# Retention attention with a mixture of experts: turned rows sent two chunks at a time, last outputs evicted by ScalarE alone, leftover rows turned in TensorE's waits, both quarters of w1 fetched ahead of x

## The chip, the cores and the metric

The kernel runs on one core of one Trainium2 chip. The metric is the device time of an execution in microseconds (us), the median of several runs. Before the change it is 405.49 us, median of 3 runs (405.27 to 405.95).

## What is computed

The reference is a chunk of recurrent attention with a decay for each head, and behind it a layer of eight experts that each take exactly 384 of the 3072 tokens.

```python
# B, H, S, D = 4, 8, 768, 64
for t in range(S):
    state = gamma[None, :, None, None] * state + einsum('bhd,bhe->bhde', k[:, :, t], v[:, :, t])
    y[:, :, t] = scale * einsum('bhd,bhde->bhe', q[:, :, t], state)
x = y.transpose(0, 2, 1, 3).reshape(3072, 512)
...
# N, D, E, F = 3072, 512, 8, 1024; cap = 384
logits = x @ w_gate
order = argsort(-logits.flatten())     # greedy: best (token, expert) pair first
for idx in order:                      # a token goes to an expert that has room
    ...
for e in range(E):
    mask = assigned == e
    out[mask] = relu(x[mask] @ w1[e]) @ w2[e]
```

## The kernel before, in words

**Stage 1, attention (0 to about 86 us).** The sequence is cut into 6 chunks of 128 tokens; a unit is one batch entry and one chunk, unit i = b + 4c, 24 in all. Groups of units (four single ones, then pairs, numbered g = 0 to 13) go through `scores`, `outputs`, `mix` and `states`. `mix` ends with the unit's output in PSUM, `yp`, channels on partitions and tokens along the free axis, and evicts it into `ys`: ScalarE (ACT) alone for chunks 0 to 4 (L419), ScalarE for one half and VectorE (DVE) for the other in the last chunk (L416, L417). Two things use `ys`. `gate(c)` multiplies the four units of a chunk with the gate's weights (L496, 32 matmuls) and ScalarE copies the logits to `gs` (L498). And the rows of x have to stand in DRAM, in `xs`, token by token, from where the experts gather them.

**Turned rows.** Units 0 to 16 (TURNED = 17) are turned by VectorE in blocks of 32 x 32 (`block_rows`, L466), so many behind each group as the table BLOCKS says, and sent by SyncE (SP): `send` (L473) issues four transfers, one for each 32 partitions. Chunks 0 to 2 of a batch entry lie in one buffer `x4` and go together (`send_long`, 16 transfers of 192 KB behind group 10), units 12 to 16 one by one (`send_one`, 20 transfers of 64 KB). Units 17 to 23 are turned by TensorE (`row_part`, L441, four 128 x 128 transposes into PSUM), evicted by ScalarE into one of four buffers `xr` (`row_out`, L449 and L451), and sent by SP as one transfer of 256 KB (L453): three of them by `early_rows`, around the last gate, and four by `rows_out`, behind the first step of the search.

**Stage 2, the choice of expert 0 (about 86 to 100 us).** For the last chunk the gate's logits are turned back (L630), VectorE takes each token's best expert (`m`, `oh`), compares with a grid of 64 thresholds (`cmp`), TensorE counts tokens over each threshold (pairs of columns, `by_two`), and VectorE narrows the grid twice, then finds the threshold (`code`, `Wq`) and the list of the expert's tokens (`idx`). `fill` issues matmuls on constants (L706) in TensorE's waits, FILL = (4, 7) of them in two places.

**Stage 3, the experts (from about 100 us).** GpSimd (POOL) issues indirect transfers in program order on one queue: the first quarter of expert 0's w1 half 0 (`fetch_first(0)`, L981, 0.5 MB) as soon as the expert is known, the three gathers of x (`fetch_x`, L989, 128 rows each) when `idx` is known and all rows are in DRAM, the second quarter (`fetch_first(1)`, L981), w1's half 1 (`fetch_w`, L950, 1 MB), then w2's halves (L950). TensorE turns the gathered rows (`turn_x`, L1002, tiles `pt` and `py`); ScalarE and VectorE split each operand into a high part (`xh` L1007, `w1h` L968) and a rest (`xlo`, `w1l`; every VectorE operation of a helper has line L152). `mm1` makes eight blocks f of the hidden layer (L1052, the first two of expert 0 in thirds by `by_thirds`, L1031; blocks f0 to f3 need w1's half 0, f4 to f7 half 1), `hh` and `hl` are their split results (ACT L1057, DVE), and `mm2` makes the output (L1074).

The search for the next expert goes on beside the matmuls. The order of each engine's instructions in this stage is set when the program is built by a planner: `Beside` and `Feed` keep estimated clocks for PE, DVE and POOL (`clk`), and after each group of matmuls decide which step of the search, which split of a weight and which transfer comes next. Engines then run strictly in that order.

## Time and profile before

| what | value |
|---|---|
| median of 3 runs | 405.49 us (405.27 to 405.95) |
| the profiled execution's own time | 405.79 us |
| its span, first to last instruction | 404.1 us |
| PE busy | 387.8 us, 96% of the span |
| DVE, ACT, POOL busy | 274.8, 156.6, 146.8 us |
| mean granted TensorE clock | 0.997 of full speed |

The profile is of one execution. It lies 0.30 us over the median, and 1.7 us of its time lie outside the span. PE is TensorE's matmuls, PEld its loads of weights, DVE VectorE, ACT ScalarE, POOL GpSimd, SP SyncE. The timeline's rows give start, length, engine, line, operation, tiles, and in brackets how long the engine had been idle and what ended that. A busy PE is not a PE at work on something needed: the constant matmuls of `fill` count as well.

### The profile page before, as it was taken

How to read it: one execution, taken by the hardware profiler on the slowest of the kernel's cores; microseconds unless marked ns; L12 is line 12 of the kernel's file. 1: busy time of each engine (PE TensorE's matmuls, PEld its weight loads, DVE VectorE, ACT ScalarE, POOL GpSimd, SP SyncE). 2: the span in 40 equal slices, each digit the busy share in tenths (PEclk: the TensorE clock that was granted, in tenths of full speed). 3: DMA queues.
4: the chain of work that ended last, by engine and by line, in shares of the span. 5: the costliest groups of instructions: out<-in, count | busy, mean ns of one | idle time of the engine just before them, and what ended most of it. 6: DMA issues, size and time to landing. Idle time of an engine off the chain costs nothing.

```text
span 404.1 us, 8464 instructions
## 1 busy us (share of the span) xinstructions
PE 387.8 (96%) x3452; PEld 338.4 (84%) x3453; DVE 274.8 (68%) x643; ACT 156.6 (39%) x287; POOL 146.8 (36%) x164
## 2 busy tenths in 40 slices
PE   8999999987989999999999999999999999999994
PEld 6989989964778889889988997898799889889982
DVE  5459767978979579867968895896688157156300
ACT  1422424233463265137315533353454265156210
POOL 5488783201600730161161451352256128021011
PEclk9999999999999999999999999999999999999998
DMA  7999988957753570375357373177146405710001
GB/s 282 423 415 423 401 290 263 243 128 252 219 225 104 171 298 1 116 246 213 104 148 295 131 255 161 55 222 271 53 156 226 165 33 180 334 54 26 2 26 60
DMA packets 22968, 77.50 MB, mean 192 GB/s; under 512 B 2693, under 2 KB 11655, under 8 KB 16393
## 3 DMA queue, kind: packets, MB, share of 16 engines
q0 software_dynamic: 8592, 46.14, 32.5%
q1 hardware_dynamic: 14330, 30.74, 21.3%
q8 instruction: 29, 0.48, 0.5%
q14 instruction: 17, 0.14, 0.1%
HBM read 64.29 MB, written 12.58 MB: 190 GB/s over the span
## 4 chain that ended last, share of the span: by engine, by line
PE 59%; issue 14%; DVE 12%; DMA 7%; POOL 4%; ACT 2%; POOLq 0%; SPq 0%; ACTq 0%; DVEq 0%
PE py L1074 24%; PE ph L1052 19%; DMA ld<-qkv 5%; PE yp L411 4%; PE sc L366 4%; DMA wraw<-w,wix 2%; PE pt L1002 2%; PE yp L396 2%; PE psm L152 2%; PE TP L430 1%; DVE w1l L152 1%; DVE w2l L152 1%; DVE cmp L152 1%; POOL out L1086 1%; DVE hl L152 1%
## 5 line engine op out<-in xcount | busy, mean ns | idle before, releaser
L1052 PE MATMUL ph<-xlo,w1h 128*128 128x384 f32 x256 | 81.8, 336 | 0.2 <-DVE xlo L152 0.2
L1052 PE MATMUL ph<-xh,w1h 128*128 128x384 f32 x248 | 81.8, 343 | 0.1
L1052 PE MATMUL ph<-xh,w1l 128*128 128x384 f32 x256 | 81.5, 335 | 0.0
L1074 PE MATMUL py<-w2h,hh 128*128 128x512 f32 x192 | 78.4, 408 | 0.0
L1074 PE MATMUL py<-w2l,hh 128*128 128x512 f32 x192 | 75.2, 392 | 0.4 <-DVE w2l L152 0.4
L1074 PE MATMUL py<-w2h,hl 128*128 128x512 f32 x192 | 75.1, 391 | 0.0
L1086 POOL DMA_INDIRECT out<-yo,oix x24 | 27.9, 1164 | 111.0 <-ACT yo L1084 99.7
L1057 ACT ACTIVATE hh<-ph 128x384 fp32r<-128x384 f32 x64 | 31.4, 490 | 62.0 <-PE ph L1052 61.3
L950 POOL DMA_INDIRECT wraw<-w,wix x31 | 36.4, 1175 | 43.6 <-DVE un L152 30.0
L1052 PEld LDWEIGHTS ph<-xh,w1h 128*128 128x128 f32 x248 | 46.3, 188 | 4.3 <-issue 2.7
L152 DVE TENSOR_TENSOR w1l<-wraw,w1h 128x1024 fp32r<-128x1024 f32 (+1 forms) x36 | 39.3, 1102 | 14.1 <-ACT w1h L968 14.0
L152 DVE SCALAR_TENSOR_TENSOR hl<-ph,hh 128x384 fp32r<-128x384 f32 x64 | 34.9, 553 | 19.7 <-ACT hh L1057 19.1
L1052 PEld LDWEIGHTS ph<-xlo,w1h 128*128 128x128 f32 x256 | 47.7, 188 | 0.5 <-DVE xlo L152 0.5
L1052 PEld LDWEIGHTS ph<-xh,w1l 128*128 128x128 f32 x256 | 47.6, 188 | 0.0
L989 POOL DMA_INDIRECT xg<-xs,idx x24 | 29.1, 1212 | 43.0 <-issue 32.6
L369 DVE TENSOR_TENSOR am<-sc,dm 128x512 f32<-128x512 f32 x48 | 30.0, 682 | 20.4 <-PE sc L366 20.4
L1074 PEld LDWEIGHTS py<-w2h,hl 128*128 128x128 f32 x192 | 36.1, 188 | 7.7
L1074 PEld LDWEIGHTS py<-w2l,hh 128*128 128x128 f32 x192 | 36.2, 188 | 7.1 <-DVE w2l L152 1.3
L1074 PEld LDWEIGHTS py<-w2h,hh 128*128 128x128 f32 x192 | 36.2, 188 | 5.8
L152 DVE TENSOR_TENSOR w2l<-wraw,w2h 128x1024 fp32r<-128x1024 f32 x32 | 38.6, 1218 | 1.6 <-ACT w2h L968 1.6
L1084 ACT ACTIVATE yo<-py 128x512 f32<-128x512 f32 x23 | 13.8, 600 | 60.5 <-PE py L1074 45.3
L968 ACT ACTIVATE w1h<-wraw 128x1024 fp32r<-128x1024 f32 (+1 forms) x36 | 33.5, 955 | 8.2 <-DMA wraw<-w,wix 8.2
(181 smaller groups left out, 546.7 us busy)
## 6 DMA issues: line engine op xcount, KB each, us to landing
ld<-qkv SPq DMA_DIRECT2D x20, 1024.0 KB, 12.0
ld<-qkv SPq DMA_DIRECT2D x4, 768.0 KB, 5.6
xs<-x SPq DMA_DIRECT2D x16, 192.0 KB, 4.6
xs<-xr SPq DMA_DIRECT2D x7, 256.0 KB, 2.6
xs<-x SPq DMA_DIRECT2D x20, 64.0 KB, 1.8
wraw<-w,wix POOLq DMA_INDIRECT x33, 7.7
xg<-xs,idx POOLq DMA_INDIRECT x24, 3.6
out<-yo,oix POOLq DMA_INDIRECT x24, 3.1
```

Of the source, the lines that this page charges most:

```text
L152: return f(o, *a, **k)
L366: nc.tensor.matmul(sc[s][:, pr, :], k_[r, w], q_[r, w], start=True, stop=True)
L369: masked.append(nc.vector.tensor_tensor(am[:, s], sc[s], dm[:, s], op=OP.mult))
L411: nc.tensor.matmul(yp[o:o + 64, pr, :], values(u)[:, 2 * pr + s, :], st[u][0][:, s, pr, :], start=(not c and pr == 0), stop=(pr == HP - 1) ...
L950: nc.gpsimd.indirect_dma_start(out=t, out_offset=None, in_=w1v if nm == "w1" else w2v, in_offset=bass.IndirectOffsetOnAxis(ap=wix[:, hf:hf ...
L968: nc.scalar.activation(p[0], p[2], AF.Copy)
L989: nc.gpsimd.indirect_dma_start(out=t, out_offset=None, in_=xs, in_offset=bass.IndirectOffsetOnAxis(ap=found[n][0][:, j:j + 1], axis=0))
L1052: nc.tensor.matmul(ph, a[:, o:o + 128], x_[:, d], start=(k == 0 and not begun), stop=(k == len(prods) - 1), skip_group_check=begun)
L1057: nc.scalar.activation(hh[:, f], ph, AF.Relu)
L1074: nc.tensor.matmul(py, h_[:, f, t], a[:, o:o + DM], start=(k == 0), stop=(k == 23))
L1084: nc.scalar.activation(yo, py, AF.Copy)
L1086: sct = nc.gpsimd.indirect_dma_start(out=out, out_offset=bass.IndirectOffsetOnAxis(ap=oix[:, j:j + 1], axis=0), in_=yo, in_offset=None, bo ...
```

## The change

It does these things:

1. The last chunk's outputs are evicted by ScalarE alone, one instruction of 128 x 512 for each unit, in place of a half by ScalarE and a half by VectorE.
2. Four chunks of a batch entry (units 0 to 15) go in buffers of two chunks: `send_two` issues 32 transfers of 128 KB, all behind group 10; unit 16 goes alone, in four of 64 KB. SP's sends stay 36 in number, with the same bytes. BLOCKS moves VectorE's turning forward: four units behind group 10, one behind group 12.
3. The rows of units 17 to 23 come from one generator, `rows_left`, in steps of two transposes; the first two units use PSUM tiles `yp`, the others `ph` and `py`. Steps are placed around the last gate and, by STEPS = (7, 1, 2), behind three steps of the first search. FILL falls from (4, 7) to (2, 7).
4. Both quarters of w1's half 0 are fetched by POOL as soon as the expert is known, ahead of the gathers of x; the first has a buffer of its own, `raw0`.
5. The four matmuls of block f0 on the first 128 rows move ahead of the second `turn_x`, and for the search of expert 1 VectorE, not ScalarE, negates the counts (`ng`).
6. The planner, with other clocks at its start, puts some later splits, transposes and transfers at other places.

```diff
--- before.py
+++ after.py
@@ -39,7 +39,7 @@
 WARM = (12, 0, 6)
 KNOWN = 3
 ROWBUFS = 4
-LONG = 3
+LONG = 4
 TURNED = 17
 GUESS = 4
 WINDOW = 6
@@ -48,12 +48,12 @@
 DEEP = 8
 LATER = (3, 4, 5)
 EVEN = 6
-BLOCKS = {g: 2 for g in (4, 5, 6, 7, 8, 9, 10, 12)}
-SEND = 10, 12
-COLD = 0
+BLOCKS = {4: 2, 5: 2, 6: 2, 7: 2, 8: 2, 9: 2, 10: 4, 12: 1}
+SEND = 10
+STEPS = 7, 1, 2
 HOT = 18
 THIRDS = 2
-FILL = (4, 7)
+FILL = (2, 7)
 READY0 = 0
 BITS = (6, 6, 5, 5, 5, 5)
 SHIFT = tuple(32 - sum(BITS[:i + 1]) for i in range(len(BITS)))
@@ -282,6 +282,7 @@
                   start=start, stop=stop)
+    raw0 = ctx.enter_context(tc.tile_pool(name="w0", bufs=1)).tile([128, 1024], F32, name="wraw0")
     yctx = ExitStack()
     yk = yctx.enter_context(tc.tile_pool(name="yk", bufs=1, side="right"))
     xo = yctx.enter_context(tc.tile_pool(name="xo", bufs=ROWBUFS, side="right"))
@@ -412,11 +413,7 @@
                                      start=(not c and pr == 0), stop=(pr == HP - 1), skip_group_check=True)
             YS[b, c] = (yk.tile([128, HP, C], F32, name=f"ys{b}_{c}") if b + B * c >= TURNED else
                         yk.tile([128, HP, C], F32, name="ys", bufs=9))
-            if c == NC - 1:
-                nc.scalar.activation(YS[b, c][:, 0:2], yp[:, 0:2], AF.Copy)
-                nc.vector.tensor_copy(YS[b, c][:, 2:4], yp[:, 2:4])
-            else:
-                nc.scalar.activation(YS[b, c], yp, AF.Copy)
+            nc.scalar.activation(YS[b, c], yp, AF.Copy)
     def states(us):
@@ -452,15 +449,15 @@
         t0 = (b * NC + c) * 128
         nc.sync.dma_start(xs[t0:t0 + 128, :], xr)
-    x4, x1 = {}, {}
+    x2, x1 = {}, {}
     def block_rows(i):
         b, c = units[i]
-        if not c:
-            x4[b] = rc.tile([128, LONG, 4, HP, 32], F32, name=f"x4{b}")
         if c < LONG:
-            x = x4[b][:, c]
+            if not c % 2:
+                x2[b, c // 2] = rc.tile([128, 2, 4, HP, 32], F32, name=f"x{b}_{c}")
+            x = x2[b, c // 2][:, c % 2]
         else:
             x = x1[i] = rw.tile([128, 4, HP, 32], F32, name="x1", bufs=TURNED - B * LONG)
         nc.vector.transpose(x.rearrange("p t d r -> p d t r"), YS[b, c].rearrange("p d (t r) -> p d t r", t=4))
@@ -472,21 +469,27 @@
         for g in range(4):
             nc.sync.dma_start(xv[b, g ^ 2 * (b % 2), :, 4 * c0:4 * c0 + x.shape[1]], x[32 * g:32 * g + 32])
-    def send_long():
-        for b in range(B):
-            send(b, 0, x4[b].rearrange("p c t d r -> p (c t) (d r)"))
+    def send_two():
+        for c in range(0, LONG, 2):
+            for b in range(B):
+                send(b, c, x2[b, c // 2].rearrange("p c t d r -> p (c t) (d r)"))
     def send_one(i):
         send(*units[i], x1[i].rearrange("p t d r -> p t (d r)"))
     written = []
-    def early_rows(k):
-        for i in range(len(written), len(written) + k):
-            pr_ = rp.tile([128, DM], F32, name="sc", bufs=4)
-            row_part(pr_, i, 0, HP)
+    def rows_left(tile_of):
+
+        while len(written) < len(units):
+            i = len(written)
+            pr_ = tile_of[0](i)
+            row_part(pr_, i, 0, 2)
+            yield
+            row_part(pr_, i, 2, HP)
+            written.append(i)
             row_out(pr_, i)
-            written.append(i)
+            yield
     def gate(c):
@@ -609,30 +612,30 @@
                 block_rows(len(written))
             if g > B:
                 next(chosen, None)
-            if g == SEND[0]:
-                send_long()
-            if g == SEND[1]:
-                for i in range(B * LONG, len(written)):
-                    send_one(i)
+            if g == SEND:
+                send_two()
         pc = rp.tile([128, 2 * E], F32, name="sc", bufs=4)
         early = [b * NC + c for c in (0, 2) for b in range(B)]
         for k, c in enumerate(early):
             by_two(pc, cmp0, oh0, c, k == 0, False)
         while len(written) < TURNED:
             block_rows(len(written))
-        for i in range(B * LONG + B, TURNED):
+        for i in range(B * LONG, TURNED):
             send_one(i)
-        early_rows(1)
+        left_over = [lambda i: rp.tile([128, DM], F32, name="yp", bufs=2)]
+        rows = rows_left(left_over)
+        next(rows)
         c = NC - 1
         gate(c)
-        early_rows(1)
+        next(rows)
         lt = rp.tile([128, 512], F32, name="sc", bufs=4)
         nc.tensor.transpose(lt[:, 0:128], gs[c % 2], ident)
         cols, Lc = slice(c, COLS, NC), lt[:, 0:128].rearrange("p (b x) -> p b x", b=B)[:, :, 0:E]
         f = best(Lc, cols, m0, oh0)
         reach(cols, B, m0, cmp0, th0)
         f()
-        early_rows(1)
+        next(rows)
+        next(rows)
         for b in range(B):
             by_two(pc, cmp0, oh0, b * NC + NC - 2, False, b == B - 1)
         n0 = other_half(pc, nc.vector)
@@ -762,7 +765,7 @@
                 sg = sgs[i]
                 if n or i:
                     yield
-                    pc, ng = count_pairs(cmp, oh, None if n else ve)
+                    pc, ng = count_pairs(cmp, oh, None if n > 1 else ve)
                     if n:
                         yield clk.pe + hear() + COPIED
                     full(pc, ng, sg)
@@ -792,7 +795,7 @@
             sel = sw.tile([128, COLS], BF, name="sel")
             ve.tensor_scalar(sel, a, code, None, op0=OP.is_equal)
             ve.scalar_tensor_tensor(Wq[:, 0:COLS], m, tv, sel, op0=OP.is_ge, op1=OP.mult)
-        if n == 0 and sent:
+        if n == 0:
             fill(FILL[0])
         ve.tensor_tensor_scan(Sc[:, 1:COLS + 1], Wq[:, 0:COLS], zer[:, 0:COLS], 0.0, op0=OP.add, op1=OP.add)
         wix = weight_rows(code, n)
@@ -800,9 +803,8 @@
         if n == 0:
             wix4 = mp.tile([128, 2], I32, name="wix4")
             ve.scalar_tensor_tensor(wix4, code.to_broadcast([128, 2]), -512.0, c_("wrow4"), op0=OP.mult, op1=OP.add)
-            raw["w1", 0, 0] = mp.tile([128, 2048], F32, name="wraw", bufs=5)
-            firsts["w1"] = wix4
             fetch_first(0, wix4)
+            fetch_first(1, wix4)
         if not last:
             both = sw.tile([128, 1], F32, name="both")
             ve.tensor_reduce(both, eh, axis=AX.X, op=OP.add)
@@ -817,7 +819,7 @@
         ve.scalar_tensor_tensor(s0, rk[:, 0:COLS], 32.0, Wq[:, 0:COLS], op0=OP.add, op1=OP.mult)
         if not last:
             ve.scalar_tensor_tensor(bad, rk[:, COLS:], float(CAP), bad, op0=OP.not_equal, op1=OP.max)
-        if n == 0 and sent:
+        if n == 0:
             fill(FILL[1])
         V, low = high_slots(s0, 1, n, None if n else nc.scalar)
         ob = low_slots(low)
@@ -962,7 +964,10 @@
             held.discard((nm, hf, e))
         s = slice(c0, c0 + w)
         hi, lo = wt[nm, hf]
-        return hi[:, s], lo[:, s], raw[nm, hf, e][:, s]
+        src = raw[nm, hf, e]
+        if isinstance(src, tuple):
+            src = src[c0 // 1024]
+        return hi[:, s], lo[:, s], src[:, s]
     def high_w(p):
         nc.scalar.activation(p[0], p[2], AF.Copy)
@@ -979,7 +984,7 @@
     def fetch_first(k, wix4):
         booked(("w1", 0, 0), 1456)
         nc.gpsimd.indirect_dma_start(
-            out=raw["w1", 0, 0][:, 1024 * k:1024 * k + 1024], out_offset=None,
+            out=raw["w1", 0, 0][k][:, 1024 * k:1024 * k + 1024], out_offset=None,
             in_=w1.rearrange("r (h x) -> (r h) x", h=4),
             in_offset=bass.IndirectOffsetOnAxis(ap=wix4.bitcast(U32)[:, k:k + 1], axis=0))
@@ -1091,19 +1096,6 @@
             scat.append(sct)
             yield 690
-    sent = []
-
-    def rows_out():
-        for i in range(len(written), len(units)):
-            pr_ = pp.tile([128, DM], F32, name="py" if i % 2 else "ph", bufs=2 if i % 2 else 3)
-            ns = 430 if i < len(written) + COLD else 220
-            row_part(pr_, i, 0, 2)
-            yield ns
-            row_part(pr_, i, 2, HP)
-            row_out(pr_, i)
-            yield ns
-        sent.append(True)
-
     class Beside:
@@ -1132,18 +1124,20 @@
             while n not in found:
                 self.step()
+    raw["w1", 0, 0] = raw0, mp.tile([128, 2048], F32, name="wraw", bufs=5)
     clk.dve = clk.pe = clk.pool = clk.dma = 0
     clk.busy.clear()
     side = Beside()
-    side.step()
-    for ns in rows_out():
-        side.tick(ns, -2)
+    left_over[0] = lambda i: pp.tile([128, DM], F32, name="py" if i % 2 else "ph", bufs=2 if i % 2 else 3)
+    for k in STEPS:
+        side.step()
+        for _ in range(k):
+            next(rows, None)
     side.finish(0)
     yctx.close()
     mq = ctx.enter_context(tc.tile_pool(name="mq", bufs=1, side="right", reuse_waits="tile"))
     for j in range(KT):
         fetch_x(0, j)
-    fetch_first(1, firsts.pop("w1"))
     fetch_w("w1", 1, 0, found[0][1])
     for _ in range(4):
         side.step()
@@ -1153,12 +1147,12 @@
         high_w(p)
     lows = []
     for j in range(KT):
+        if j == 1:
+            by_thirds(0, range(1))
         turn_x(0, j, lows)
-        if not j:
-            pass
-        else:
+        if j:
             side.step()
-            by_thirds(j - 1, range(THIRDS))
+            by_thirds(j - 1, range(1 if j == 1 else 0, THIRDS))
         if j < KT - 1:
             low_w(quarters[j])
         lows.pop(0)[1]()
```

On POOL, from expert 0's first weight transfer to expert 1's first (`wraw` is a weight's buffer, `xg` gathered rows, `out` the scatter of results). Before:

```order
L981 DMA wraw<-w,wix_1673 128x1024
L989 DMA xg<-xs,idx 128x512 x3
L981 DMA wraw<-w,wix_1673 128x1024
L950 DMA wraw<-w,wix 128x2048
L1170 COPY spacer<-xh 1x1
L950 DMA wraw<-w,wix 128x2048 x3
L989 DMA xg<-xs,idx 128x512 x2
L1085 MEMSET spacer 1x1
L1086 DMA out<-yo,oix 3072x512
L989 DMA xg<-xs,idx 128x512
L950 DMA wraw<-w,wix 128x2048 x2
```

After the change:

```order
L986 DMA wraw_95<-w,wix_1663 128x1024
L986 DMA wraw<-w,wix_1663 128x1024
L994 DMA xg<-xs,idx 128x512 x3
L952 DMA wraw<-w,wix 128x2048
L1164 COPY spacer<-xh 1x1
L952 DMA wraw<-w,wix 128x2048 x3
L994 DMA xg<-xs,idx 128x512
L1090 MEMSET spacer 1x1
L1091 DMA out<-yo,oix 3072x512
L994 DMA xg<-xs,idx 128x512 x2
L952 DMA wraw<-w,wix 128x2048
```

The second row of the quarters stands ahead of the three gathers instead of behind them, so w1's half 1 (L952 there, L950 before) comes directly behind the gathers; of expert 1's gathers one, instead of two, stands ahead of the first scatter.

On ACT, from expert 0's gathered rows to its first blocks of the hidden layer (`w1h_1792` and `w1h_1790` are half 0, `w1h_1897` and `w1h_1888` half 1). Before:

```order
L968 ACTIVATE w1h_1792<-wraw 128x512 x2
L1007 ACTIVATE xh<-pt 128x4x128 x2
L218 ACTIVATE ng<-psm 64x8
L1007 ACTIVATE xh<-py 128x2x128 x2
L968 ACTIVATE w1h_1792<-wraw 128x512 x2
L1057 ACTIVATE hh<-ph 128x384
L968 ACTIVATE w1h_1897<-wraw 128x512 x2
L1057 ACTIVATE hh<-ph 128x384
L968 ACTIVATE w1h_1897<-wraw 128x512
L1057 ACTIVATE hh<-ph 128x384
```

After the change:

```order
L973 ACTIVATE w1h_1790<-wraw_95 128x512 x2
L1012 ACTIVATE xh<-pt 128x4x128 x2
L1012 ACTIVATE xh<-py 128x2x128 x2
L973 ACTIVATE w1h_1790<-wraw 128x512 x2
L973 ACTIVATE w1h_1888<-wraw 128x512
L1062 ACTIVATE hh<-ph 128x384
L973 ACTIVATE w1h_1888<-wraw 128x512
L1062 ACTIVATE hh<-ph 128x384
L973 ACTIVATE w1h_1888<-wraw 128x512
L1062 ACTIVATE hh<-ph 128x384
```

One part of half 1 stands ahead of the first `hh` (block f0) where two stood between the first and the second `hh`; `ng` is gone from ACT.

On PE, from expert 1's last turned block of rows (`pt`) to the count that narrows expert 2's grid (`psm<-sg_90`); `py` is expert 0's output, `ph` expert 1's first block. Before:

```order
L1002 MATMUL pt<-ident,xg 128x128 x4
L1074 MATMUL py<-w2h_2003,hh 128x512
L1074 MATMUL py<-w2l_2004,hh 128x512
L1074 MATMUL py<-w2h_2003,hl 128x512
L1074 MATMUL py<-w2h_2003,hh 128x512
L1074 MATMUL py<-w2l_2004,hh 128x512
L1074 MATMUL py<-w2h_2003,hl 128x512
L1052 MATMUL ph<-xh,w1h_2218 128x384 x4
L1052 MATMUL ph<-xh,w1l_2219 128x384 x4
L1052 MATMUL ph<-xlo,w1h_2218 128x384 x4
L152 LDWEIGHTS onesb
L152 MATMUL psm<-sg_90,onesb 128x8
```

After the change:

```order
L1007 MATMUL pt<-ident,xg 128x128 x4
L1057 MATMUL ph<-xh,w1h_2214 128x384 x3
L152 LDWEIGHTS onesb
L152 MATMUL psm<-sg_90,onesb 128x8
L1057 MATMUL ph<-xh,w1h_2214 128x384
L1057 MATMUL ph<-xh,w1l_2215 128x384 x4
L1057 MATMUL ph<-xlo,w1h_2214 128x384 x4
```

Six matmuls of expert 0 stood between the turned block and expert 1's first matmul, and none stand there now; the count comes behind three matmuls of expert 1 instead of twelve.

## Rows read from the trace of the kernel before

**Rows 1.** The page, part 1: busy time of each engine, share of the span, instructions.
```profile
PE 387.8 (96%) x3452; PEld 338.4 (84%) x3453; DVE 274.8 (68%) x643; ACT 156.6 (39%) x287; POOL 146.8 (36%) x164
```
**Rows 2.** Timeline of ACT: start us, us, engine, line, operation, tiles [idle before <-releaser].
```profile
75.32 0.60 ACT L419 ACTIVATE ys<-yp 128x512 f32<-128x512 f32 x1 [0.75 <-PE yp L411]
...
85.70 0.39 ACT L416 ACTIVATE ys<-yp 128x256 f32<-128x256 f32 x1 [0.50 <-PE yp L411]
```
**Rows 3.** Timeline of DVE, stage 1's end.
```profile
70.43 2.48 DVE L369 TENSOR_TENSOR am<-sc,dm 128x512 f32<-128x512 f32 x4 [2.27 <-PE sc L366]
...
87.05 0.74 DVE L417 COPY ys<-yp 128x256 f32<-128x256 f32 x2
87.72 0.70 DVE L466 STREAM_TRANSPOSE x<-ys 128x512 f32<-128x512 f32 x1
89.27 0.19 DVE L152 TENSOR_REDUCE m<-sc 128x4 f32<-128x32 f32 x1 [0.86 <-PE sc L630]
```
**Rows 4.** Timeline of PE, the gate of chunk 4 and the last one's end.
```profile
81.37 1.08 PE L496 MATMUL sc<-ys,wgf 128*32 128x128 f32 x32
...
87.52 0.95 PE L496 MATMUL sc<-ys,wgf 128*32 128x128 f32 x12 [0.32 <-DVE ys L417]
```
**Rows 5.** Timeline of SP's queue: issues of the rows' transfers, DVE's and TensorE's.
```profile
65.47 25.77 SPq L473 DMA_DIRECT2D xs<-x  x36
91.34 4.59 SPq L453 DMA_DIRECT2D xs<-xr  x7
```
**Rows 6.** Timeline of POOL, expert 0's transfers.
```profile
96.97 1.16 POOL L981 DMA_INDIRECT wraw<-w,wix  x1 [22.00 <-DVE low L152]
100.24 0.94 POOL L989 DMA_INDIRECT xg<-xs,idx  x1 [2.11 <-DVE idx L152]
...
102.74 1.13 POOL L989 DMA_INDIRECT xg<-xs,idx  x1 [0.30 <-issue]
104.18 0.94 POOL L981 DMA_INDIRECT wraw<-w,wix  x1 [0.30 <-issue]
105.42 1.45 POOL L950 DMA_INDIRECT wraw<-w,wix  x1 [0.30 <-issue]
```
**Rows 7.** From issue to landing: L981 95 to 106 us, then L950 104 to 112.
```profile
DMA to landing us min/median/max: 4.7/4.7/4.8
...
DMA to landing us min/median/max: 8.4/9.0/9.6
```
**Rows 8.** Chain that ended last, 80 to 122 us: start us, us, what.
```profile
105.42 8.96 DMA wraw<-w,wix
...
114.95 0.61 ACT w1h L968
```
**Rows 9.** Timeline of PE, expert 0's blocks f0 to f4.
```profile
109.02 0.94 PE L1052 MATMUL ph<-xh,w1l 128*128 128x384 f32 x4
...
113.99 0.46 PE L152 MATMUL psm<-oh,cmp 128*128 128x16 bf16 x12
...
116.31 0.34 PE L1052 MATMUL ph<-xh,w1l 128*128 128x384 f32 x1
118.31 0.17 PE L152 MATMUL psm<-sg,onesb 128*128 128x8 bf16 x1 [1.67 <-DVE sg L152]
```
**Rows 10.** Timelines of ACT and DVE, block f0's split and the search beside it.
```profile
110.72 0.49 ACT L1057 ACTIVATE hh<-ph 128x384 fp32r<-128x384 f32 x1 [0.65 <-PE ph L1052]
...
112.36 0.94 DVE L152 TENSOR_TENSOR cmp<-m,th 128x768 bf16<-128x768 f32 x1
```
**Rows 11.** Timeline of PE, its two longest waits in experts 0 and 1 behind that.
```profile
129.42 0.50 PE L1074 MATMUL py<-w2l,hh 128*128 128x512 f32 x1 [0.36 <-DVE w2l L152]
...
149.46 0.17 PE L152 MATMUL psm<-sg,onesb 128*128 128x8 bf16 x1 [0.93 <-DVE sg L152]
```
**Rows 12.** Windows: length, PE, PEld, DVE, ACT, POOL busy (x), granted clock, DMA share, GB/s.
```profile
92.00:96.00 4.00, 2.49 (x26) 1.59 (x26) 3.28 (x16) 1.97 (x6) 0.00 (x0) 1.00 0.96 352
...
402.00:404.10 2.10, 0.00 (x0) 0.00 (x0) 0.00 (x0) 0.00 (x0) 0.00 (x0) 0.50 0.02 8
```

## The prediction

> **What bounds the kernel now.** I read the page first. PE is busy 387.8 of 404.1 us [rows 1]: whatever does not shorten PE's waits, or start its long run of expert matmuls earlier, is worth nothing. Next I looked for the waits in the timeline of PE, and followed the chain of waits back from the largest. From about 118 us to the end PE waits almost nowhere: 0.36 and 0.93 us are the two longest [rows 11]. So the change can only earn between the last outputs (86 us) and expert 0's fifth block (118 us), and the quantity to forecast is the start of block f4, 118.34 us now, directly behind the count at 118.31 [rows 9].
>
> Three pieces set it.
>
> (a) The last gate. ACT begins its half of the last unit at 85.70 and is done at 86.09 [rows 2]. DVE reaches its halves of the last two units at 87.05 and ends them at 87.79 [rows 3], because it does other work first. The gate's last 12 matmuls wait for them and end at 88.47 [rows 4], and DVE, after 0.86 idle, can look at the logits only at 89.27 [rows 3]. From there a dependent chain leads to the list of tokens and to the first gather at 100.24 [rows 6].
>
> (b) POOL. It issues one gather or quarter each 1.25 us (100.24 to 102.74 for two), the last gather at 102.74, then the second quarter at 104.18, and only at 105.42 w1's half 1 [rows 6].
>
> (c) That transfer. It takes 8.96 us, to 114.38, and stands in the chain that ended last; ACT splits its second part from 114.95 [rows 8]. ACT's next `hh`, DVE's `hl` and its splits are queued behind, and so the count of expert 1's search, for which PE idles 1.67 us [rows 9].
>
> **The change, part by part.**
>
> Eviction by ACT alone: a full 128 x 512 eviction lasts 0.60 [rows 2], so the last unit is ready at 85.70 + 0.60 = 86.30. Only the gate's matmuls on the three earlier units can start before that; 29 of 32 are left, 29/32 x 1.08 = 1.0 [rows 4], end about 87.35 against 88.47: **1.1 us earlier**. DVE loses its copies, and of the three transposes that it still had at the end (0.70 each, [rows 3]) two move behind group 10, where it idles 2.27 us [rows 3]: 1.4 us fit. Without that cover they would delay masked scores by 1.4; it is the one cost I set to nothing on this ground. The logits come at 88.15, the list 1.1 earlier, and the first gather at about 99.1. The generator's row steps (`yp`, `ph`, `py`) are the same transposes in smaller pieces; PE is busy 2.49 of 4 us there [rows 12], so they hide in its waits. `ng` on DVE is one small instruction in place of one on ACT, below 0.2, and no one waits for it at once.
>
> Sends: 36 issues took SP 25.77 us, to 91.24, partly waiting for late transposes, and the seven `xr` transfers stood behind them (91.34 + 4.59 = 95.93) [rows 5]. 32 transfers of 128 KB and 4 of 64 KB carry the same bytes but no longer wait for units 13 to 15. The last `xr` can be no later than now in any case, and now it holds no one: gathers wait for the list [rows 6]. With the list 1.1 earlier, `xr` has to move too; its last eviction does, since it follows PE and ACT and no longer SP. I cost it at nothing; its bound is the 1.1 that would be lost again.
>
> Fetch order: quarter 1 leaves the place between gathers and half 1. One POOL issue is 1.25 (105.42 - 104.18 = 1.24). Half 1 is issued at 105.42 - 1.1 - 1.25 = **103.07**. In front of the gathers the quarters need two issues from about 95.9 (96.97 - 1.1) to 98.4, before the first gather at 99.1: 0.7 to spare.
>
> When does half 1 land? A quarter takes 4.7 from issue to landing, the halves 8.4 to 9.6 with transfers around them [rows 7]. At 103.07 both quarters (98.4 at latest + 4.7 = 101.9 to 103) are in, so only the gathers are still under way. Bounds: 103.07 + 4.7 = 107.8 and 103.07 + 8.96 = 112.0. I take 109.9, the middle, for it is twice a quarter's bytes but without a quarter ahead of it.
>
> What does f4 make of it? In the new order of ACT one part of half 1 stands ahead of the first `hh`. That `hh` starts at 110.72 now [rows 10] and could at 109.5 (all moved 1.2: 1.1 from the chain and 0.1 from block f0's four matmuls moved ahead). From `hh` to the counted pairs: 0.49 + 0.54 + 0.94 [rows 10] and a hand-over, 2.1; the pairs stand at 113.99 on PE [rows 9], 112.8 then. So `hh` may wait to 110.7 before PE notices, and the split ahead of it takes about 0.6: half 1 may land as late as **110.1** at no cost. Up to there PE runs f0 to f3 without a wait, and the 1.67 goes as well: f4 at 118.34 - 1.2 - 1.67 = 115.5. Behind 110.1 each us of landing costs one.
>
> What is late next: DVE's split of w2 (0.36) and expert 1's count (0.93) [rows 11]. At expert 1 the new order puts its first matmul directly behind the last turned block, so PE must wait for ACT's eviction, 0.60 [rows 2], and a hand-over; the count then waits less, since it stands ahead of DVE's work. 0.7 for 0.93 with a possible eviction of outputs queued before it (0.60 more): between -0.3 and +0.4. I take zero for that and for the 0.36, and +-0.5 for the planner's many small moves in experts 2 to 7, which no row of before prices.
>
> **The sum.** -1.2 - 1.67 = -2.9 us against the profiled execution's 405.79: 402.9. That execution is 0.30 over the median of 405.49, so the median after is 405.49 - 2.9 = **402.6 us**.
>
> **A rule against it.** In the windows between gate and gathers PE is busy 2.49 of 4 us and the granted clock stays 1.00, its 2.4 GHz level; it is at 0.50, the 1.2 GHz level, only behind the last matmul, with PE idle [rows 12]. Two constant matmuls fewer leave PE a little more idle there, and row steps fill part of it; I price it at nothing, and the opposite case is the fourth rival. The Trainium skill ("TensorE: Matmul & The Clock Gate", What's actually happening) says that the clock is halved when the engine has been too little busy, so by this rule fewer fills could cost the clock just ahead of expert 0.
>
> **Rivals.**
>
> 1. *The weight is late again.* Half 1 lands at 112.0 (8.96 as now, because the transfers behind it share the engines as before). For it: all three halves took 8.4 or more [rows 7]. Against: each of those had another half or a quarter in flight. f4 then comes 1.9 later: a gain of 1.0, 404.5 us. Chance 0.17.
>
> 2. *Quarter 2 is held on POOL.* POOL started the first quarter at 96.97, with its idle time ended by DVE's `low`, an instruction the quarter does not need [rows 6]. If a second issue among DVE's dense work waits like this until DVE has the list, the gathers go back to 100.2 and half 1 to 104.2, landing between 108.9 and 113.2: no gain from the chain, 1.67 or nothing from the stall, 403.8 to 405.5. Chance 0.07. The Trainium skill has the mechanism ("DMA: Bandwidth & Descriptors", SWDGE vs HWDGE vs iDMA): GpSimd writes descriptors into SBUF, from which VectorE's fast modes can lock it out; the row of 96.97 agrees.
>
> 3. *Slower: `hh` queued behind a late weight.* Before, the first `hh` stood ahead of half 1 in ACT's order; now it stands behind. If half 1 lands no earlier than now, 114.4, `hh` of f0 to f3 all stand behind it, DVE's comparison and the pairs follow 2.1 + 0.6 later, at 117.1 instead of 112.8, and f4 at 115.5 + 4.3 = 119.8: 1.5 later than now, 407.0. It is slower from a landing at about 112.9 on. For it: both quarters, the gathers and the last rows now share the DMA engines (share 0.96 at 92 to 96 us, [rows 12]). Against: it needs 11.3 us where 9.6 is the longest seen [rows 7]. Chance 0.06; another 0.03 I give to new waits in the later experts that sum to 4 us.
>
> 4. *The clock falls* to its lower level [rows 12] for one window's length around expert 0's start: 4 us of work take 4 us more, +4 - 2.9, 406.6. Chance 0.02.
>
> 5. *The change does not act*: the gate is not earlier since PE or DVE arrives there no sooner, and half 1 is off the path. 405.4. Against: the row at 87.52 names DVE's `ys`. Chance 0.03.
>
> **How the numbers follow.** Forecast 0.62: 402.6, with its bounds for the later waits and the landing 401.4 to 404.0. A measurement of this kernel can tell 0.2%, 0.8 us, from no change, so faster means below 404.7. Faster: 0.62 + 0.14 of the first rival + 0.03 of the second = 0.79. Slower (above 406.3): 0.06 + 0.03 + 0.02 = 0.11. Same: the rest of both and the fifth, 0.03 + 0.04 + 0.03 = 0.10. The range goes from 401.4 to 404.9: it takes in the first rival and leaves out the cases behind it and a larger gain, together under 0.2.
>
> **What would show it.** Right: gate's end near 87.4, first logits read at 88.2, first gather at 99.1, both quarters issued by 98.4, half 1 issued at 103 and landed by 110, no wait of PE at the count before f4, f4 at 115.5. Wrong: a gather that waits for the rows' writes or for POOL; `hh` of f0 ended by a weight's transfer; new waits over 0.9 in experts 1 to 7; or PE's granted clock under 1.00 anywhere between 86 and 398 us.

## The result and the profile after

The kernel became slower: median 409.97 us over 22 executions, against 405.27 us of the kernel before in as many; the ratio is 1.008, 95% interval 1.0052 to 1.0109. Forecast were 402.6 us and a range from 401.4 to 404.9. The executions fall into groups by the mean clock that each of them lists for TensorE: 7 at 0.995 or more took 405.24 to 406.30 us, 3 at 0.990 to 0.991 took 407.5 to 409.4, and 11 at 0.986 or less 410.0 to 411.4. (The ratio leaves out two executions as slow, one of 765.58 us at full clock, whose cause is not known, and that of 411.35.) So two things are to be explained: why most executions run at a lower clock, and why even those at full clock gain nothing: the median of the seven is 405.91.

The profiled execution is of the first group: 406.22 us, span 404.5, clock 0.995. First the timeline of PE, which answers to [rows 4, 9]:

```profile
84.95 0.42 PE L438 MATMUL yp<-ident,ys 128*128 128x128 f32 x2
85.30 1.27 PE L499 MATMUL sc<-ys,wgf 128*32 128x128 f32 x32
...
97.47 4.04 PE L709 MATMUL py<-zer,onesb 128*128 128x512 bf16 x18
103.22 0.66 PE L1007 MATMUL pt<-ident,xg 128*128 128x128 f32 x4 [1.70 <-DMA xg<-xs,idx]
104.61 0.67 PE L1036 MATMUL ph<-xh,w1h 128*128 128x128 f32 x4 [0.74 <-ACT xh L1012]
105.11 0.62 PE L1007 MATMUL pt<-ident,xg 128*128 128x128 f32 x4
...
116.06 0.33 PE L1057 MATMUL ph<-xh,w1h 128*128 128x384 f32 x1
...
116.58 0.18 PE L152 MATMUL psm<-sg,onesb 128*128 128x8 bf16 x1
...
124.70 0.39 PE L1079 MATMUL py<-w2h,hh 128*128 128x512 f32 x1
...
144.80 0.79 PE L1057 MATMUL ph<-xh,w1h 128*128 128x384 f32 x3 [0.69 <-ACT xh L1012]
...
219.35 0.79 PE L1057 MATMUL ph<-xh,w1h 128*128 128x384 f32 x3 [0.74 <-ACT xh L1012]
...
239.50 0.50 PE L1079 MATMUL py<-w2l,hh 128*128 128x512 f32 x1 [0.71 <-DVE w2l L152]
242.50 0.50 PE L1079 MATMUL py<-w2l,hh 128*128 128x512 f32 x1 [1.35 <-DVE w2l L152]
```

And the rows of the kernel before that answer to these and stand in no group:

```profile
55.30 0.85 PE L496 MATMUL sc<-ys,wgf 128*32 128x128 f32 x19 [0.70 <-issue]
...
99.37 4.04 PE L706 MATMUL py<-zer,onesb 128*128 128x512 bf16 x18
103.51 0.66 PE L1002 MATMUL pt<-ident,xg 128*128 128x128 f32 x4
...
126.95 0.39 PE L1074 MATMUL py<-w2h,hh 128*128 128x512 f32 x1
```

The gate ends at 86.57, 1.9 us earlier than before, and needs no wait. The 18 constant matmuls behind the search's last step start 1.9 earlier as well and end at 101.51. Then PE has nothing: 1.70 us for the first gather, and 0.74 for ACT's eviction of the first turned block. The count no longer waits, but stands at 116.58 instead of 118.31 [rows 9]. It no longer stands directly ahead of f4: a block is twelve matmuls, f3's begin at 113.88, and so f4 begins at 116.06, three matmuls ahead of the count, and not at 115.5. And there are new waits in expert 3, one at its first block (219.35) and two at its output. POOL's timeline, the answer to [rows 6]:

```profile
94.39 1.16 POOL L986 DMA_INDIRECT wraw<-w,wix  x1 [20.26 <-DVE un L152]
95.85 1.05 POOL L986 DMA_INDIRECT wraw<-w,wix  x1 [0.30 <-issue]
98.33 0.94 POOL L994 DMA_INDIRECT xg<-xs,idx  x1 [1.42 <-DVE idx L152]
...
102.27 0.94 POOL L952 DMA_INDIRECT wraw<-w,wix  x1 [0.30 <-issue]
```

And from issue to landing, the answer to [rows 7]: both quarters together (L986), the first gather (L994), w1's half 1 (L952), and last the first gather of the kernel before (L989):

```profile
DMA to landing us min/median/max: 4.8/5.7/6.6
...
DMA to landing us min/median/max: 4.8/4.8/4.8
...
DMA to landing us min/median/max: 6.6/6.6/6.6
...
DMA to landing us min/median/max: 3.2/3.2/3.2
```

POOL is on time everywhere. But the second quarter, issued at 95.85, lands 6.6 us later, at 102.5, and the first gather, issued at 98.33, behind it at 103.2: 4.8 us instead of 3.2. Half 1 is the good surprise: 6.6 us, at 108.9.

### The profile page after: what moved, and what is told of

The parts are those of the page before. It is cut to its first block, busy times and chain, and to the rows that moved or that the text cites. A ratio compares the mean times of both kernels' runs of the same rounds, so it can differ in the third digit from the quotient of the medians.

```text
span 404.5 us, 8462 instructions
## 1 busy us (share of the span) xinstructions
PE 387.0 (96%) x3450; PEld 337.2 (83%) x3451; DVE 274.0 (68%) x641; ACT 156.8 (39%) x285; POOL 145.6 (36%) x164
## 4 chain that ended last, share of the span: by engine, by line
PE 70%; issue 14%; DVE 6%; DMA 3%; POOL 3%; ACT 2%; SPq 0%; POOLq 0%; DVEq 0%; ACTq 0%
PE ph L1057 26%; PE py L1079 23%; PE yp L412 5%; PE sc L367 5%; PE yp L397 2%; PE TP L427 2%; PE pt L1007 2%; PE psm L152 2%; DMA ld<-qkv 2%; PE sc L499 2%; POOL out L1091 1%; DVE w2l L152 1%; POOL wraw L952 1%; DVE am L370 1%; PE ph L1036 1%
## 5 line engine op out<-in xcount | busy, mean ns | idle before, releaser
L952 POOL DMA_INDIRECT wraw<-w,wix x31 | 35.9, 1157 | 40.4 <-DVE un L152 32.3
L994 POOL DMA_INDIRECT xg<-xs,idx x24 | 28.6, 1190 | 51.7 <-issue 32.8
```

What stands on the lines that cost most here:

```text
L952: nc.gpsimd.indirect_dma_start(out=t, out_offset=None, in_=w1v if nm == "w1" else w2v, in_offset=bass.IndirectOffsetOnAxis(ap=wix[:, hf:hf ...
L994: nc.gpsimd.indirect_dma_start(out=t, out_offset=None, in_=xs, in_offset=bass.IndirectOffsetOnAxis(ap=found[n][0][:, j:j + 1], axis=0))
```

## The experiments

All were compared with the kernel before on the same chip; the ratio is to that. Experiments 7, 8 and 11 ran on another chip than `hot28`, so their distance from it is one between two ratios. (On one chip, that of `swap`, `swap600` and the two edits of the kernel before, the kernel before itself took 408.8 us.)

**1. The change again.**

> The changed kernel as it is. Theory: two things eat the gain, and they add up. (1) In the expert stage the planner's order of expert 3 leaves two waits of PE for DVE's w2l, 0.71 and 1.35 us; they are there in every execution. (2) In some executions the granted clock of TensorE is lower (mean 0.983 to 0.986 instead of 0.995), and these take 409.4 to 411.4 us, the others 405.2 to 407.8; it falls because PE now has nothing to do between its constant matmuls' end at 101.5 and the first gathered rows at 103.2. So: again two groups of times, near 406 and near 410, each with its clock, and a mean clock 0.01 lower wherever the time is 4 us longer. Rival: the times spread without a second level of the clock; then it is contention, not the clock.

Ratio 1.0079 (1.0048 to 1.0111), median 409.3. Six of 12 executions at clock 0.979 to 0.984 took 409.9 to 412.3 us, three at 0.995 to 0.999 took 405.3 to 406.1, three at 0.990 to 0.991 lay between. The groups go with the clock. The profiled execution is one of those between (406.59 us, 0.991). Its clock stays at 1.00 behind the wait for the first gather (1.42 us), but is 0.50 from 94 to 97 us: a second, shorter fall, in which the seven constant matmuls of the search take 3.15 us instead of 1.67. The two others between have no profile.

**2. A longer cover for the wait.**

```diff
-HOT = 18
+HOT = 28
```

> 28 instead of 18 constant matmuls ahead of the first gathered rows, so that PE works on until about 103.6 us; the planner's order is unchanged. Theory (idle PE lets the clock fall): no execution near 410 any more, mean clock 0.995 or more in all of them, median 405.5 to 406.5, 0.4 us later at the first turned rows at most. Rival (the clock falls for another reason, the two constant matmuls fewer in the search at 92 us, or something outside this stage): the group near 410 stays, at clock 0.983 to 0.986, and the median is within 0.5 us of the unchanged kernel's.

Ratio 1.0025 (1.0013 to 1.0037): all 12 between 406.02 and 407.20 us, none below clock 0.995. The group near 410 is gone. The median, 406.63, is just over what was expected. The timeline of PE in this kernel:

```profile
97.86 6.20 PE L709 MATMUL py<-zer,onesb 128*128 128x512 bf16 x28
103.90 0.60 PE L1007 MATMUL pt<-ident,xg 128*128 128x128 f32 x4
```

And its windows, with the columns of [rows 12]:

```profile
100.00:104.00 4.00, 4.00 (x20) 1.91 (x19) 3.85 (x11) 0.33 (x1) 2.99 (x3) 1.00 0.67 187
104.00:108.00 4.00, 3.27 (x39) 3.02 (x37) 2.51 (x5) 1.55 (x4) 0.00 (x0) 1.00 0.84 280
```

The rows come no sooner, and are turned 0.4 us behind their landing (98.72 + 4.8 = 103.5), but PE is busy all of 100 to 104 us and the clock stays at 1.00 there. (The shorter fall of experiment 1 is in this execution too, 0.73 and 0.84 in the two windows from 92 to 100.) The wait of 0.73 for `xh` is still there and alone lets nothing fall behind it.

**3. The same idle time in the kernel before.**

```diff
-HOT = 18
+HOT = 8
```

> The kernel before with 8 instead of 18 constant matmuls ahead of the gathered rows, nothing else: PE idles for about 2.2 us there, from 101.2 to the rows at 103.5. Theory (this idle time lets the clock fall, change or no change): a group of executions 4 to 5 us longer, about 410, at mean clock 0.983 to 0.988, the others at 405.5. Rival (it takes something of the change): one group, 405.0 to 406.5.

Ratio 1.0092 (1.0068 to 1.0116): all six executions at 0.976 to 0.978, 412.2 to 413.7 us on the chip where the kernel before takes 408.8: 3.7 longer by the medians, and in all of them where some were expected. The wait in its profile is 2.39 us for the first gather and 0.78 for the second. The change has no part in this kernel; idle PE alone does it. Its windows:

```profile
100.00:104.00 4.00, 1.61 (x8) 0.64 (x7) 3.65 (x14) 1.15 (x2) 2.96 (x3) 1.00 0.38 95
104.00:108.00 4.00, 3.22 (x29) 2.93 (x29) 4.00 (x9) 1.37 (x3) 2.46 (x3) 0.72 0.75 216
108.00:112.00 4.00, 4.00 (x21) 4.00 (x20) 0.87 (x4) 1.69 (x4) 1.77 (x3) 0.50 0.77 249
112.00:116.00 4.00, 4.00 (x15) 4.00 (x15) 2.94 (x6) 0.86 (x2) 0.32 (x1) 0.50 0.95 367
116.00:120.00 4.00, 4.00 (x35) 3.84 (x34) 3.38 (x7) 2.59 (x7) 0.00 (x0) 1.00 0.47 197
```

PE idles in 100 to 104, and the clock goes to 0.50, the 1.2 GHz level, behind it, when PE is busy 4.00 of 4 us again. (This execution has two more falls, 0.64 at 96 to 100 and 0.80 and 0.78 from 216 to 224.)

**4. The constant matmuls of the search put back.**

```diff
-FILL = (2, 7)
+FILL = (4, 7)
```

> The changed kernel with four constant matmuls again in the first place of the search, 18 ahead of the gathered rows as in the change. Theory (the long fall of the clock hangs on the wait for the first gather, not on the search): the two groups stay, about half of the executions 3 to 5 us longer than the others at a mean clock of 0.982 to 0.991, ratio to the kernel before 1.004 to 1.010. Rival (two constant matmuls fewer at 92 us let the clock fall): one group at the level of hot28, ratio 1.001 to 1.0035.

Ratio 1.0061 (1.0027 to 1.0095): six executions at 405.4 to 406.2, six at 409.0 to 412.8. The two matmuls fewer are not the cause.

**5. The second quarter behind the gathers again.**

```diff
             fetch_first(0, wix4)
-            fetch_first(1, wix4)
...
         fetch_x(0, j)
+    fetch_first(1, firsts.pop('w1'))
     fetch_w("w1", 1, 0, found[0][1])
```

> The changed kernel with the second quarter of w1 fetched behind the three gathers again, as in the kernel before; the order of every other instruction is that of the change. Theory: in the changed kernel the first gather, issued at 98.33, lands only at 103.17 because 1 MB of weights stands ahead of it in POOL's queue (second quarter landed at 102.50), and so PE idles and the clock falls. Without it the gather takes 3.2 to 3.5 us and lands near 101.5, where the 18 constant matmuls end: no execution near 410, PE's first turned rows near 101.6 instead of 103.2, f4 near 115.3 instead of 116.6 although w1's half 1 is issued 1.25 later, median 404.5 to 405.5. Rival (the gathers are late because the rows' writes or the DMA engines are busy): landing still 4.5 us or more behind the issue, two groups of times as before.

Half a miss.

```profile
98.52 0.95 POOL L994 DMA_INDIRECT xg<-xs,idx  x1 [3.27 <-DVE lim L152]
...
101.92 0.66 PE L1007 MATMUL pt<-ident,xg 128*128 128x128 f32 x4 [0.71 <-DMA xg<-xs,idx]
```

The gather is no longer late: its rows are turned 3.4 us behind its issue, and PE waits 0.71 instead of 1.70. But the lower clock stays (seven of 12 at 0.974 to 0.987, where none of the kernel before on this chip was under 0.988), ratio 1.0076 (1.0046 to 1.0106). In the profile two waits are left, 0.71 and 0.74 for `xh`, and the clock is 0.53 in 104 to 108 us behind them. The quarter is one part of the idle time, not all of it: here the gather is issued 0.75 us behind the end of `idx` (97.77), in the change 0.26 (98.07), and the trace names another instruction of DVE, `lim`. That is 0.49 of the 0.71; why the gather waits for it is not known.

**6. Both quarters ahead of the gathers in the kernel before.**

```diff
             fetch_first(0, wix4)
+            fetch_first(1, wix4)
...
-    fetch_first(1, firsts.pop("w1"))
```

> The kernel before with the second quarter of w1 ahead of the gathers, nothing else. Theory: the first gather, issued at about 100.2, lands 4.5 us or more later instead of 3.2, so PE idles 1.3 us or more behind its constant matmuls; some executions at a clock of 0.983 to 0.988, 409 or more; w1's half 1 is issued 1.25 earlier, which takes up to 1.2 us of the 1.67 us wait at the count, so the other executions are at 404.5 to 405.5. Rival (the fetch order is what gains and something else lets the clock fall): one group at 404 to 405.

Ratio 0.9995 (0.9969 to 1.0021). Three of 12 executions at 0.981 to 0.986 took 412 to 414 us where the others took 406.3 to 409.3. In its profile, at full clock from 100 us on, PE waits 0.77 for the first gather and no longer waits for the count ahead of f4:

```profile
103.86 0.66 PE L1002 MATMUL pt<-ident,xg 128*128 128x128 f32 x4 [0.77 <-DMA xg<-xs,idx]
...
124.82 0.39 PE L1074 MATMUL py<-w2h,hh 128*128 128x512 f32 x1
```

The gather, issued at 99.90, took 3.9 us and not the 4.5 that were expected. From its issue to expert 0's output it is 24.9 us (124.82 - 99.90) and in the kernel before 26.7 (126.95 - 100.24): this order of fetches alone gives 1.8 us in expert 0, and with it the idle time.

**7. Block f0's four matmuls behind the second turned block again** (on top of `hot28`).

```diff
-        if j == 1:
-            by_thirds(0, range(1))
         turn_x(0, j, lows)
...
-            by_thirds(j - 1, range(1 if j == 1 else 0, THIRDS))
+            by_thirds(j - 1, range(THIRDS))
```

> hot28 (28 constant matmuls, so that the clock stays) with block f0's four first matmuls behind the second turned block again, as in the kernel before. In the changed kernel they stand between the first and the second turned block and wait 0.7 us for ACT's eviction, while the second gather has landed. Theory: that place costs; the third turned block comes 0.5 to 0.9 us earlier (105.9 to 106.3 us instead of 106.8), the rest behind it too: 0.1 to 0.2% less than hot28, a ratio of 1.000 to 1.0015 to the kernel before. Rival (PE has slack there, the end of f0 is set by the third gather or by DVE's splits): no change, 1.0025.

Ratio 1.0008 (0.9993 to 1.0024), 0.17% below `hot28`; the intervals overlap, but the trace has it: both blocks are turned in a row at 103.70 (the first in `hot28` at 103.90), the third at 105.98 instead of 106.98, and the count behind it is at 108.18 instead of 109.18. Without the 0.20 at the start it is 0.8 us.

**8. The last outputs in halves again** (on top of `hot28`).

```diff
-            nc.scalar.activation(YS[b, c], yp, AF.Copy)
+            if c == NC - 1:
+                nc.scalar.activation(YS[b, c][:, 0:2], yp[:, 0:2], AF.Copy)
+                nc.vector.tensor_copy(YS[b, c][:, 2:4], yp[:, 2:4])
+            else:
+                nc.scalar.activation(YS[b, c], yp, AF.Copy)
```

> hot28 with the last chunk's outputs in halves by ScalarE and VectorE again, nothing else. Theory (the gate's gain of the prediction is real, 1.1 us): last gate's end 1.1 us later, the first gather's issue 1.1 later, and the time 0.6 to 1.1 us longer than hot28, a ratio of 1.004 to 1.0055; less than 1.1 since the constant matmuls end 0.1 behind the landing there. Rival (the two transposes moved on DVE made the gain, not the eviction): gate's end less than 0.5 later, no change of the time.

Ratio 1.0045 (1.0026 to 1.0065), 0.2% above `hot28`; here too the intervals overlap, and the trace decides. The timeline of PE, of this kernel:

```profile
85.52 0.36 PE L152 MATMUL sc<-oh,cmp 128*128 128x16 bf16 x8
86.88 0.44 PE L442 MATMUL yp<-ident,ys 128*128 128x128 f32 x2 [0.99 <-DVE ys L418]
87.25 1.08 PE L503 MATMUL sc<-ys,wgf 128*32 128x128 f32 x32
```

From the pairs' start to the gate's end it is 88.33 - 85.52 = 2.8 us, and in `hot28` 1.8 (84.49 to 86.32): the eviction by ACT alone gives 1.0.

**9 to 11. The planner's order.** All edits add time to its clock of PE; the first two at expert 0, the third at expert 1.

```diff
-    clk.pe = max(clk.pe, arrive["x", KT - 1, 0] + 2500)
+    clk.pe = max(clk.pe, arrive["x", KT - 1, 0] + 4000)
```

> The planner's clock of PE starts expert 0 at 4000 instead of 2500 ns behind the last gather, which gives experts 3 to 7 almost the order of the kernel before (two splits of w2 ahead of expert 3's last blocks instead of one); all up to expert 0's second block is the same. Theory (order costs 2.1 us in every execution): both groups of times shift down by 1.5 to 2.5 us, to about 404 and 408, and PE no longer waits for w2l at expert 3's output. Rival (the waits are a consequence of running ahead, and PE waits elsewhere for the same transfer or engine): less than 0.7 us of shift.

Median 407.6, ratio 1.0027 (0.9998 to 1.0057). Six executions at 404.2 to 406.8, six at 0.984 to 0.986 with 408.4 to 409.5: both groups about 1 to 1.7 us below those of the change, of 1.5 to 2.5 expected. The waits for `w2l` are gone from the list of PE's waits, but 1.2 us for DVE's `hl` are new in expert 0. The profiled execution is one with the lower clock, and shows best where it falls. PE's timeline:

```profile
97.58 4.04 PE L709 MATMUL py<-zer,onesb 128*128 128x512 bf16 x18
103.60 0.66 PE L1007 MATMUL pt<-ident,xg 128*128 128x128 f32 x4 [1.98 <-DMA xg<-xs,idx]
104.99 1.12 PE L1036 MATMUL ph<-xh,w1h 128*128 128x128 f32 x4 [0.74 <-ACT xh L1012]
```

And the windows of the same execution:

```profile
100.00:104.00 4.00, 2.02 (x12) 0.94 (x10) 3.86 (x11) 0.60 (x2) 2.71 (x3) 1.00 0.69 213
104.00:108.00 4.00, 3.26 (x27) 2.96 (x26) 1.62 (x4) 1.20 (x2) 0.00 (x0) 0.60 0.80 263
108.00:112.00 4.00, 4.00 (x21) 4.00 (x21) 1.60 (x5) 2.21 (x5) 1.67 (x3) 0.50 0.04 12
112.00:116.00 4.00, 4.00 (x17) 4.00 (x18) 3.44 (x7) 0.77 (x2) 0.43 (x1) 0.62 0.96 354
116.00:120.00 4.00, 4.00 (x35) 3.69 (x34) 3.58 (x10) 2.65 (x6) 0.00 (x0) 1.00 0.40 168
```

L1036's four matmuls last 1.12 there and 0.67 at full clock. The clock that is missing is 4 x (0.40 + 0.50 + 0.38) = 5.1 us of work, some 10 us at the lower level, beside 4 us between the groups.

The second has this edit and HOT = 28:

> Both edits. If both theories hold: one group of times, 403.0 to 404.3, all at clock 0.995 or more, faster than the kernel before by 0.3 to 0.6%. If the clock does not hang on the constant matmuls: two groups near 404 and 408.

Ratio 0.9995 (0.9979 to 1.001): one group, 404.5 to 406.8, but not as low as expected, for this order has the wait for `hl` (1.6 us in this profile). The third keeps the change's expert 0:

```diff
     for n in range(E):
+        if n == 1:
+            clk.pe += 600
         feed.expert(n)
```

> hot28 and 600 ns on the planner's clock at expert 1, which gives experts 2 to 7 the order of the kernel before. Theory (the waits for w2l at expert 3's output, 2.1 us, come from the planner's order alone): they vanish, ratio 0.997 to 0.9985, some 404.5 us against 405.6. Rival: PE waits elsewhere for the same splits, ratio 1.001 or more.

Ratio 0.9958 (0.9938 to 0.9977), 0.67% below `hot28`, some 2.7 us (1.8 to 3.6 by the ends of the two intervals). In its profile the two waits for `w2l` are gone, and so is that of 0.74 for `xh` at expert 3's first block: 2.8 us of waits in `hot28`, against some 0.7 that are new elsewhere.

One more run (`swap600`) has this edit and that of experiment 5 together, with HOT = 18. Expected were one group and 0.5 to 0.8% less than the kernel before, and it was a miss: ratio 1.0013 (0.9984 to 1.0042), mean clocks from 0.985 to 0.997. In its profile the waits for the first gather and for `xh` are 0.78 and 0.74 us, and the clock stays at 1.00 behind them. But PE waits 1.01 for the count ahead of f4 and 2.24 for `xlo` in expert 1, and there the clock falls:

```profile
144.00:148.00 4.00, 1.55 (x8) 0.81 (x7) 2.42 (x3) 2.37 (x5) 1.02 (x1) 0.98 1.00 418
148.00:152.00 4.00, 3.53 (x11) 3.22 (x12) 2.10 (x4) 1.37 (x2) 0.00 (x0) 0.50 0.46 186
```

**12. Quarter, place and order undone together**, with HOT = 21 and the edits of 5, 7 and 11.

> What stays of the change when the parts that seem to cost are undone together: second quarter behind the gathers, f0's matmuls behind the second turned block, 21 constant matmuls, the planner's clock as in hot28_600. Theory: first turned rows at 101.9, a short wait for the second gather as in the kernel before (0.9), f4 at 114.8 to 115.6, no lower clock, ratio 0.992 to 0.995, 402.5 to 403.5 us. Rival (w1's half 1, issued 1.25 us later, lands behind 110 and the wait at the count before f4 comes back): f4 at 116.5 or later, ratio 0.996 to 0.999.

Ratio 0.9974 (0.9946 to 1.0002), within the rival's range: no low clock (0.992 at least), first rows at 102.35, but the wait at the count is back (0.92, at 117.07). The chain of this execution shows that half 1 is behind it, issued at 105.40 and landed at 112.83, 2.7 us later than 110.1:

```profile
105.40 7.43 DMA wraw<-w,wix
112.83 0.02 issue
112.85 1.15 ACT w1h L973 x2
```

**13. The three costs taken out**: HOT = 28, and the edits of 7 and 11; both quarters stay in front.

> The change with its three costs taken out together: 28 constant matmuls, block f0's matmuls behind the second turned block, 600 ns on the planner's clock at expert 1; both quarters stay ahead of the gathers. Theory (the savings of hot28_late, 0.17%, and of hot28_600, 0.67%, add up): ratio 0.993 to 0.996, 402.5 to 404.2 us where the kernel before takes 405.6. Rival (they meet in the same wait at expert 1's third turned block): the ratio of hot28_600, 0.9958, or more.

Ratio 0.9935 (0.9913 to 0.9956): six executions at 401.94 to 402.75 us, clock 0.995 or more. The savings add up, and this version is faster than both kernels.

## Why the prediction was wrong

**The gate: right.** Forecast 1.1 us earlier; experiment 8 gives 1.0. The profile's 1.9 has 0.84 us more that is not the change's: in the kernel before, PE lost 0.70 at 55 us with nothing that the profile shows as cause. `hot28` has no such loss, nor has the kernel before with experiment 6's edit, and in both the pairs ahead of the gate stand at 84.49.

**The fetch order: the step that failed.** "In front of the gathers the quarters need two issues [...], before the first gather at 99.1: 0.7 to spare." That counted POOL's time for issuing and not the megabyte that then stands in front of the gather in the same queue. POOL had its time; the gather took 4.8 us to land instead of 3.2. The whole gain of the gate was used up there: the gather was issued 1.9 us earlier (98.33 against 100.24), but PE's first turned rows came 0.3 earlier (103.22 against 103.51). In the other traces that name this landing with both quarters ahead it is 4.2 to 5.5 us. Whether the gather waits its turn in the queue or shares the DMA engines with the quarter, no run tells apart. The second rival, quarter 2 held on POOL, named the right effect, no gain from the chain, for a reason that the rows of POOL refute: the second quarter was issued 0.30 behind the first.

**Half 1 and the wait before f4: right.** It landed at 108.9 by a forecast of 109.9, under the 110.1 that were free, and the 1.67 us wait is gone. f4 came 2.3 us earlier (116.06 against 118.34) instead of 2.8, and 0.84 of that is the one above: 1.4 are the change's, for the chain's 1.2 were missing. The sum did not see that three matmuls of f4 would stand ahead of the count. Four matmuls of f0, which I counted as 0.1 of gain, cost 0.7 to 0.8 (experiment 7): they wait for ACT, and the second block's turning, whose rows had landed, waits behind them.

**The planner's order: priced at 0.5 us either way, cost 2.8.** "+-0.5 for the planner's many small moves in experts 2 to 7, which no row of before prices." At expert 3 one split of w2 instead of two stands ahead of its last blocks, and PE waits 0.71 and 1.35. Its first block stands directly behind a turned block, as at expert 1, and PE waits 0.74 for ACT's eviction; at expert 1 I had priced this at 0.7, and it was 0.69. The orders of both kernels show that, and I had read only those of experts 0 and 1. Experiments 9 and 11 move the order alone; both take the waits for `w2l` away, and 11 leaves expert 0 as it is. The two profiles add up: the change is 2.25 us ahead at expert 0's output (124.70 against 126.95), 1.5 ahead where expert 3's begins (237.03 against 238.56), and its span is 0.4 longer.

**The clock: the fourth rival, with 2 chances in 100, in about half of the executions or more.** Its price of +4 us, for 4 us of work at the lower level, came near the 4.9 between the medians of the highest and the lowest clock group; the profiles have 5.1 missing. I had it hang on the two constant matmuls of the search, which experiment 4 acquits. It hangs on the wait that the fetch order opened: constant matmuls that covered all of it before (ended 103.41, rows at 103.51) end 1.7 us too early. Covering it ends the low group (experiment 2); opening it in the kernel before lowers the clock in all six executions (3). By the Trainium skill ("TensorE: Matmul & The Clock Gate", What's actually happening) a TensorE that had too little to do goes to half its clock; the runs agree in that 0.50 follows the idle time in experiments 3 and 9.

So at full clock the change's gains (gate and half 1) are eaten by the queue, by a wait in PE's order and by the planner; the clock makes it slower. Why only some executions fall is open: the work is the same in all of them. The wait for the first gather was 1.42 and 1.70 us in two profiles in which the clock stayed and 1.98 and 2.32 (experiments 9 and 4) in two in which it fell, but its size alone does not decide: behind 0.71 it fell (experiment 5), and behind 0.78 it stayed (`swap600`).

## What to carry to other kernels

A transfer that moves ahead in a queue can delay the landing of what stands behind it, and not only its issue (here by 1.0 to 2.3 us for 0.5 MB, and by 0.7 in experiment 6): price it by landing times. Where constant matmuls cover a wait, any change of the chain ahead of it changes what they cover; look at where they end and where the data land, and cover with some to spare. When a planner sets the order, read the new order of every stage for the splits that a matmul waits for, before calling its moves small.

## What the runs showed that was not expected

A wait of PE of 1.7 and 0.7 us cost 4 to 5 us, for the clock stayed at 0.50 for about 10 us, in most of which PE was busy 4.00 of 4 us. The clock that is missing there is 5.1 us of work in each of the four profiles with this fall (experiments 3, 4, 5 and 9). A wait of 0.73 us alone cost no clock in 12 executions (experiment 2). And w1's half of 1 MB, issued as the quarter in front of it landed, took 6.6 us to its own landing, where it had taken 8.96 [rows 8] and takes 7.43 with the second quarter just in front of it (experiment 12).
